# The rows of twelve k transfers and of a table divided anew among sixteen DMA engines, in a fused linear attention and spectral mixing kernel

## The chip, the cores and the metric

The kernel runs on one core of a Trainium2 chip. The core has a matrix engine (PE, with its weight loads PEld), a vector engine (DVE), a scalar engine (ACT), GpSimd (POOL) and SyncE (SP), and sixteen DMA engines that move data between HBM and on-chip memory. Time is device microseconds (us) of one execution, the median of several.

## The reference

For 8 batches, 8 heads, 576 positions and a head width of 64 (model width 512), in float32:

```python
def phi(x):
    return np.where(x > 0, x, np.exp(x) - 1.0) + 1.0
kv  = einsum('bhsd,bhse->bhde', phi(k), v);  z = phi(k).sum(over positions)
x   = einsum('bhsd,bhde->bhse', phi(q), kv) / (einsum('bhsd,bhd->bhs', phi(q), z) + 1e-6)
# heads side by side: x is (8, 576, 512)
X   = rfft(x, over positions);  Y = 0
Y[:, :64] = complex product of X[:, m] with (w_r[m] + i*w_i[m]) for the 64 lowest modes m
u   = x + irfft(Y)
out = u + maximum(u @ w_ch, 0)
```

w_r and w_i are 64 matrices of 512 x 512 each, so the weights are 134 MB of float32; q, k and v are 9.4 MB each. The output is 9.4 MB.

## The kernel before

**Stage one: attention and the forward transform.** For each batch `load(b)` (L172) brings q, k and v as one 128-row tile each: row r holds 2 x 1152 float32 numbers, converted to float16 on the way, so each row lands as two pieces of 2304 bytes. All of them but q of batch 0 go out on POOL's queue. `exps` (ACT) and `features` (DVE) form phi, `turn_q` and `sum_kv` (PE) transpose q and sum k times v, `form_x` divides by the denominator, and `transform` and `place_x` make the 64 modes. `load(b + 2)` is called at the top of batch b, and each of the tags q16, k16 and v16 has two buffers, so the loads of batch b + 2 wait until batch b has used its tile.

**The table.** The cosine and sine table is not loaded whole: FROWS = 576 // 4 - 63 = 81 of its rows come from HBM on SP's queue (L182), and `fold_table` (L330) makes rows 64 to 127 and a fifth block from rows 0 to 80 with matmuls whose k range is `slice(0, FROWS)`. Each row of the transfer is 4 x 128 float16, 1024 bytes.

**Weights.** `w_load` (L99) brings two modes of w_r and two of w_i in turn as 128 rows of 32 KB float32, which land as 16 KB bfloat16, on POOL's queue too. The first goes out in two halves of 64 rows between the loads of batches 3 and 5 (`next(pending)`, L467), four more follow the loads of batch 7, then the 512 x 512 matrix w_ch (`wch16`, L657), then one at a time, each when the PE has finished with the buffer that it takes (L106, two buffers of tag "w" and three of "wp"). `w_load_last` (L115) cuts the last modes into pieces, the last of them 64 KB.

**Stage two: one matrix pair after the other.** `mode_block(p)` multiplies the modes of all batches with weight tile p (L525, sixteen matmuls of 128 x 512), and between these blocks the PE and the other engines do rows of the inverse transform, the channel product and so on out of a list of work (`work_slot`).

**The end.** `last_pair` (L626) takes the last pieces as they land (L644). After them come a short chain of transposes, matmuls and copies (L1185 to L1210) and the last sums of each output tile (L1043), with stores on SP's queue.

**What the steps of the change touch.** `SHARES` (L170) says how a k tile's 128 rows are cut into transfers: batch 3 into 15, 63 and 50 rows, batch 5 into 5, 77, 35 and 11, every other tile into one transfer of 128. The loop at L186 issues one transfer per part. L68 and L182 set the table's rows.

Of the kernel before, what the change touches and what calls it, by code (L numbers as in the profile page):

```python
# [20 lines left out]
def _dft_consts(S: int, NM: int):  # L21

    m = np.arange(NM)
    s_cols = np.concatenate([4 * np.arange(128) + jj for jj in range(4)] + [512 + np.arange(NP)])
    s_rows = np.concatenate([s_cols, s_cols[512:]]).reshape(5, 128).T
    ang = 2.0 * np.pi * s_rows[:, :, None] * m / S
    by_four = np.concatenate([m[g::4] for g in range(4)])
    fwd = np.concatenate([np.cos(ang)[:, :, by_four], -np.sin(ang)[:, :, by_four]], axis=2)

    return fwd.astype(np.float16)  # L30
# [3 lines left out]
def kernel(  # L34
# [10 lines left out]
    nc = tc.nc  # L45
# [6 lines left out]
    NJJ = 4  # L52
# [12 lines left out]

    fwd_np = _dft_consts(S, NM)
    FROWS = S // 4 - 63
    fwd_dr = nc.inline_tensor(np.ascontiguousarray(fwd_np[:FROWS, :4]), name="dft_fwd")  # L68

    const = ctx.enter_context(tc.tile_pool(name="const", bufs=1, side="right"))  # L70
    xpool = ctx.enter_context(tc.tile_pool(name="xpool", bufs=1, side="right"))
# [3 lines left out]
    fwd_sb = const.tile([128, 5, 2 * NM], F16, name="fwd_sb")  # L75
# [17 lines left out]
    pin = tc.keep_in_program_order  # L93
# [73 lines left out]

    qT_all = [q_tile(f"qT{b}") for b in range(B)]
    raw, phi, x16s, xfs = {}, {}, {}, {}
    SHARES = {("k", 3): (15, 63, 50), ("k", 5): (5, 77, 35, 11)}  # L170

    def load(b):  # L172
        for nm, src in (("q", q), ("k", k), ("v", v)):
            rows_in = src[b].rearrange("h s d -> (h s) d").rearrange(
                "(hp r j) d -> r hp (j d)", r=128, j=2 * NJ
            )
            if (nm, b) == ("q", 0):
                for c in range(2):
                    t = sA.tile([128, 2, NJ * Dh], F32, tag="x16", bufs=2, name=f"q32_{c}")
                    pin(nc.sync.dma_start(out=t, in_=rows_in[:, :, c * NJ * Dh : (c + 1) * NJ * Dh]))  # L180
                    raw[nm, b, c] = t
                pin(nc.sync.dma_start(out=fwd_sb[0:FROWS, 0:NJJ, :], in_=fwd_dr.ap()))  # L182
                continue
            t = sA.tile([128, 2, 2 * NJ * Dh], F16, tag=f"{nm}16", bufs=2, name=f"{nm}16_{b}")
            r0 = 0
            for n in SHARES.get((nm, b), (128,)):  # L186
                pin(nc.gpsimd.dma_start(out=t[r0 : r0 + n], in_=rows_in[r0 : r0 + n]))
                r0 += n
            raw[nm, b] = t
# [259 lines left out]
    def set_diagonal(k: int, of=slice(0, B), copies=(nc.vector.tensor_copy,)):  # L449
        for g in range(4):  # L450
            rows = slice(32 * g, 32 * g + 32)
            src = xt[rows, of, :, k : XK : NQ - 1].rearrange("p b c t -> p c t b")
            pin(copies[g % len(copies)](out=xz[k % 2][rows, :, :, g, of], in_=src))  # L453

    load(0)
    load(1)
    ones_where(id16, -1, 1, 0)
    make_turns()
# [4 lines left out]
    for b in range(B):  # L463
        if b + 2 < B:
            load(b + 2)
            if b % 2 == 1:
                next(pending)  # L467
            if b == 2:
                pin(nc.gpsimd.memset(xz[0], 0.0))
        turn_q(b, 0)  # L470
        turn_q(b, 1)
        if b == 0:
            fold_table()
        sum_kv(b)
        if b + 1 < B:
            for _ in features(b + 1):
                pass
        if b + 2 < B:
            exps(b + 2)
        for jj in range(NJJ + 1):  # L480
            form_x(b, jj)
            if b == 0 and jj == 0:
                make_place()
            if b > 1 and jj == 1:
                place_x(b - 2)
            if b > 0 and jj in (2, 3):
                transform(b - 1, jj - 2)
        if b > 0:
            transform(b - 1, 2)
            transform(b - 1, 3)  # L490
# [245 lines left out]
    def x_of(t: int):  # L736
        if t < B * NJJ:
            return x_main[t // NJJ][:, t % NJJ, :]
        i = t - B * NJJ
        return x_tail[i // 2][:, i % 2, :]  # L740
# [234 lines left out]
    for b in range(B):  # L975
        pairs += [(b * NJJ, b * NJJ + 1), (b * NJJ + 2, b * NJJ + 3)]
        if b % 4 == 3:
            k = b // 4
# [251 lines left out]
    for i, t in enumerate(pairs[0]):  # L1230
# [4 lines left out]
                out=x_of(t), in0=accs[0][:, i], scalar=0.0, in1=x_of(t), op0=ALU.max, op1=ALU.add  # L1235
# [60 lines left out]
```

## Time and profile before

| what | us |
|---|---|
| median of 3 runs (lowest, highest) | 417.94 (417.76, 418.09) |
| the profiled execution, in all | 417.94 |
| its span, first to last instruction | 416.2 |
| PE busy / DVE busy / ACT busy / POOL busy | 304.5 / 243.7 / 148.5 / 51.9 |
| last mark of the first weight tile in halves (batch 3 of the loads) | 43.7 |
| last mark of v of batch 7, the last q, k, v transfer | 82.3 |
| first and last mark of the last weight piece | 383.1, 386.1 |
| span after the last mark | 30.1 |

A mark is a step of a transfer's semaphore. The trace holds sixteen of them for each transfer, one for each DMA engine that finished its share. They do not carry an engine's number. It also holds each DMA packet with its start, duration, bytes and queue, again without an engine's number.

| transfer | its sixteen marks in order, us |
|---|---|
| v, batch 2 | 28.08 28.11 28.16 28.19 28.21 28.22 28.26, 28.57 28.61 28.65 28.67 28.72 28.73 28.75 28.76, 29.68 |
| v, batch 3 | 35.88 35.91 35.98 35.98 36.02 36.07, 36.47, 37.01 37.11 37.12 37.15 37.19, 38.04, 38.15, 38.78 38.91 |
| last weight piece | 383.12 383.61 384.18 384.41 384.50 384.51 384.57 384.89 384.94 385.31 385.67 385.74 385.81 385.82 385.93 386.11 |

Queue 0 in the profile is POOL's transfers, queue 1 SP's, and the two "instruction" queues bring the program itself: queue 8 in packets of 16 KB, queue 14 in packets of 8 KB. A DMA share of the span is the time of all sixteen engines together.

### The profile page before, as it was taken

How to read it: one execution, taken by the hardware profiler on the slowest of the kernel's cores; microseconds unless marked ns; L12 is line 12 of the kernel's file. 1: busy time of each engine (PE TensorE's matmuls, PEld its weight loads, DVE VectorE, ACT ScalarE, POOL GpSimd, SP SyncE). 2: the span in 40 equal slices, each digit the busy share in tenths (PEclk: the TensorE clock that was granted, in tenths of full speed). 3: DMA queues.
4: the chain of work that ended last, by engine and by line, in shares of the span. 5: the costliest groups of instructions: out<-in, count | busy, mean ns of one | idle time of the engine just before them, and what ended most of it. 6: DMA issues, size and time to landing. Idle time of an engine off the chain costs nothing.

```text
span 416.2 us, 6713 instructions
## 1 busy us (share of the span) xinstructions
PE 304.5 (73%) x2767; PEld 171.4 (41%) x2767; DVE 243.7 (59%) x542; ACT 148.5 (36%) x220; POOL 51.9 (12%) x91
## 2 busy tenths in 40 slices
PE   0269799999583466576665466988978887887993
PEld 0167677777341233233332233443433333452431
DVE  3779978995732654557474442555455644722795
ACT  4667787864300001000000112244443442322583
POOL 6233423100110000000000000000100000230200
PEclk9999955788688558666666679789999999999997
DMA  8999999999999999999999999999999999999698
GB/s 216 211 211 217 208 221 202 226 217 213 217 213 216 217 219 219 211 218 219 216 219 211 219 217 217 219 212 217 218 216 222 209 219 217 213 212 195 216 402 344
DMA packets 16652, 92.84 MB, mean 223 GB/s; under 512 B 2054, under 2 KB 2807, under 8 KB 12335
## 3 DMA queue, kind: packets, MB, share of 16 engines
q0 software_dynamic: 12816, 81.70, 94.3%
q1 hardware_dynamic: 3806, 10.73, 6.8%
q8 instruction: 21, 0.34, 0.3%
q14 instruction: 9, 0.07, 0.0%
HBM read 163.66 MB, written 9.44 MB: 416 GB/s over the span
## 4 chain that ended last, share of the span: by engine, by line
DMA 53%; PE 26%; DVE 12%; ACT 3%; issue 3%; POOL 2%; DVEq 0%; ACTq 0%; POOLq 0%
DMA w<-in_moe_w_r_dram 33%; DMA w<-in_moe_w_i_dram 16%; PE P L525 9%; PE kvp L264 5%; DVE x_main L1043 3%; DMA k<-in_k_dram 3%; DVE x L300 3%; PE qTp L244 3%; PE eps L906 2%; PE xf L434 2%; DVE xz L453 1%; PE num L158 1%; ACT qT L251 1%; ACT ke L210 1%; DVE rd L297 1%
## 5 line engine op out<-in xcount | busy, mean ns | idle before, releaser
L525 PE MATMUL P<-w,xz 128*64 128x512 bf16 x480 | 82.9, 507 | 51.6 <-DMA w<-in_moe_w_r_dram 24.6
L525 PEld LDWEIGHTS <-xz 128*64 128x64 bf16 x480 | 39.1, 138 | 84.8 <-issue 72.6
L536 ACT CAST ys<-P 128x512 f16<-128x512 f32 x8 | 4.7, 585 | 115.6 <-PE P L525 115.6
L906 PE MATMUL eps<-wch,xTw 128*128 128x512 f16 x144 | 37.5, 385 | 3.8 <-DVE xTw L898 3.8
L887 DVE TENSOR_TENSOR x_main<-ya,x_main 128x512 f32<-128x512 f32 x32 | 21.9, 688 | 28.5 <-PE ya L883 28.2
L889 ACT CAST x16w<-x_main 128x512 f16<-128x512 f32 x32 | 19.8, 618 | 44.2 <-DVE x_main L887 43.3
L453 DVE COPY xz<-xt 32x384 bf16<-32x384 bf16 (+2 forms) x62 | 31.4, 507 | 2.1 <-ACT xt L419 1.2
L264 PE MATMUL kvp<-vpad,ke 32*128 32x130 f16 x576 | 23.4, 265 | 8.3 <-ACT qT L251 8.3
L837 PE MATMUL nw<-kv_diag,qT 128*128 128x130 f16 (+1 forms) x160 | 21.7, 261 | 10.3 <-DVE x_main L850 4.4
L914 ACT CAST E<-eps 128x512 f16<-128x512 f32 (+1 forms) x40 | 21.1, 539 | 22.1 <-PE eps L906 22.1
L534 DVE CAST ys<-P 128x512 f16<-128x512 f32 x10 | 6.9, 691 | 33.3 <-PE P L525 33.3
L264 PEld LDWEIGHTS <-ke 32*128 32x128 f16 x576 | 21.8, 117 | 9.7 <-issue 9.4
L244 PE MATMUL qTp<-id,qe 128*128 128x128 f16 x144 | 16.8, 310 | 11.3 <-DVE qe L228 9.6
L106 POOL DMA_DIRECT2D w<-in_moe_w_i_dram x15 | 8.0, 532 | 136.0 <-PE P L525 82.5
L106 POOL DMA_DIRECT2D w<-in_moe_w_r_dram x16 | 8.7, 545 | 124.5 <-PE P L525 114.9
L300 DVE TENSOR_TENSOR x<-num,rd 128x512 f16<-128x512 f32 x32 | 22.1, 691 | 1.1
L837 PEld LDWEIGHTS <-qT 128*128 128x128 f16 (+1 forms) x160 | 13.3, 125 | 22.6 <-issue 13.2
L898 DVE COPY xTw<-xTp 128x512 f16<-128x512 f16 x36 | 14.9, 416 | 9.8 <-PE xTp L896 9.7
L158 PE MATMUL num<-kv_sb,qT 64*128 64x65 f16 (+1 forms) x320 | 16.1, 220 | 6.1 <-DVE x L300 3.9
L251 ACT COPY qT<-qTp 128x1152 f16<-128x1152 f16 x16 | 19.5, 1282 | 2.6 <-PE qTp L244 2.0
L244 PEld LDWEIGHTS <-qe 128*128 128x128 f16 x144 | 14.6, 146 | 12.4 <-DVE qe L228 10.0
L848 DVE RECIPROCAL rdw<-nw 128x4 f32<-128x4 f32 (+1 forms) x40 | 7.0, 176 | 20.8 <-PE nw L837 20.4
(162 smaller groups left out, 501.0 us busy)
## 6 DMA issues: line engine op xcount, KB each, us to landing
w<-in_moe_w_i_dram POOLq DMA_DIRECT2D x15, 2048.0 KB, 17.0
w<-in_moe_w_r_dram POOLq DMA_DIRECT2D x14, 2048.0 KB, 15.5
out_dram<-x_main SPq DMA_DIRECT2D x14, 512.0 KB, 3.2
v<-in_v_dram POOLq DMA_DIRECT2D x8, 576.0 KB, 14.0
q<-in_q_dram POOLq DMA_DIRECT2D x7, 576.0 KB, 12.7
k<-in_k_dram POOLq DMA_DIRECT2D x6, 576.0 KB, 12.6
w<-in_moe_w_r_dram POOLq DMA_DIRECT2D x2, 1024.0 KB, 16.6
w<-in_moe_w_r_dram POOLq DMA_DIRECT2D x4, 512.0 KB, 11.9
```

Source lines behind the costliest of these rows:

```text
L158: mm = nc.tensor.matmul(num[hpo][orow, c0 : c0 + 65], qT[rows, hpp, h2, cols], kv_sb[rows, hpp, h2, :])
L244: nc.tensor.transpose(qT_ps[:, j], phi["q", b][:, c, j].rearrange("p o d -> p (o d)"), id16,)
L251: nc.scalar.copy(out=qT[:, :, c * NJ : (c + 1) * NJ], in_=qT_ps.rearrange("p j x -> p x j"))
L264: nc.tensor.matmul(kv_ps[:, h2, 0:130], phi["k", b][r0 : r0 + 32, j // NJ, j % NJ].rearrange("p o d -> p (o d)"), vp[r0 : r0 + 32, :, j, 0 ...
L300: nc.vector.tensor_tensor(out=dst.rearrange("p (o c d) -> p o c d", o=2, c=4), in0=nv[:, :, :, 0:64], in1=rden.unsqueeze(3).broadcast_to([ ...
L453: pin(copies[g % len(copies)](out=xz[k % 2][rows, :, :, g, of], in_=src))
L525: nc.tensor.matmul(P[c : c + width, :], x, w[:, dc, :], start=first, stop=last, tile_position=(0, c), skip_group_check=True,)
L837: nc.tensor.matmul(num[c][orow, h2 * 130 : h2 * 130 + 130], qT[:, c, h2, rows_of(jj, BASE[b % 2])], kv_diag[:, b, c, h2].rearrange("p o n ...
L887: pin(nc.vector.tensor_tensor(out=x, in0=acc, in1=x, op=ALU.add))
L889: pin(nc.scalar.copy(out=x16w[t], in_=x))
L906: nc.tensor.matmul(e_ps, xT[:, c, :], wch16[:, c, :], start=(c == 0), stop=(c == NDC - 1))
L914: pin(nc.scalar.copy(out=dst, in_=e_ps[:, cols]))
```

## The change

The table's transfer takes 96 rows in place of 81 (81 rounded up to a multiple of 16). `fold_table` still reads rows 0 to 80. The k tile of batch 3 is cut into four parts (18, 6, 100, 4) in place of three, that of batch 4 into four (20, 88, 2, 18) in place of one, and that of batch 5 into four others (15, 22, 84, 7). Nothing else differs. POOL issues 90 listed operations in place of 86; SP, PE, DVE and ACT issue the same ones as before.

```diff
     FROWS = S // 4 - 63
-    fwd_dr = nc.inline_tensor(np.ascontiguousarray(fwd_np[:FROWS, :4]), name="dft_fwd")
+    LROWS = -(-FROWS // 16) * 16
+    fwd_dr = nc.inline_tensor(np.ascontiguousarray(fwd_np[:LROWS, :4]), name="dft_fwd")
...
-    SHARES = {("k", 3): (15, 63, 50), ("k", 5): (5, 77, 35, 11)}
+    SHARES = {("k", 3): (18, 6, 100, 4), ("k", 4): (20, 88, 2, 18), ("k", 5): (15, 22, 84, 7)}
...
-                pin(nc.sync.dma_start(out=fwd_sb[0:FROWS, 0:NJJ, :], in_=fwd_dr.ap()))
+                pin(nc.sync.dma_start(out=fwd_sb[0:LROWS, 0:NJJ, :], in_=fwd_dr.ap()))
```

## The prediction

> **What bounds the kernel now.** I read first the DMA rows of the page, then its queues, then who waits for whom, then the chain that ended last.
>
> ```profile
> span 416.2 us, 6713 instructions
> ...
> DMA  8999999999999999999999999999999999999698
> ...
> q0 software_dynamic: 12816, 81.70, 94.3%
> q1 hardware_dynamic: 3806, 10.73, 6.8%
> q8 instruction: 21, 0.34, 0.3%
> q14 instruction: 9, 0.07, 0.0%
> ```
>
> The sixteen DMA engines are full from the first slice to the 37th. Instruction packets are 0.3% of all DMA time, but each falls on one engine.
>
> ```profile
> POOL w L106 <- PE P L525: 197.4, 21, 26.8
> ...
> PE P L525 <- DMA w<-in_moe_w_i_dram: 25.5, 10, 6.6
> PE P L525 <- DMA w<-in_moe_w_r_dram: 24.6, 11, 4.9
> ```
>
> ```profile
> 349.37 17.05 DMA w<-in_moe_w_i_dram
> 366.46 1.93 PE P L525 x16
> 368.40 0.29 issue
> 368.69 2.73 POOL w L122 x5
> 371.41 0.19 issue
> 371.60 13.84 DMA w<-in_moe_w_i_dram
> 385.49 0.36 PE yt L644 x8
> ```
>
> ```profile
> 386.15 0.26 PE L644 MATMUL yt<-xs,w 128*128 128x16 bf16 x4
> ...
> 386.45 0.22 DVE L652 CAST Y<-yt 128x64 f16<-128x64 f32 x1 [3.01 <-PE yt L644]
> ```
>
> In the second stage the PE waits for weights (25.5 + 24.6 us), not the weights for room: POOL's long waits at L106 end well before the queue runs dry. The transfer issued at 349.37 follows one whose earliest engine ends at 353.77 (its first mark), 4.4 us later. The last four matmuls of the last weights start at 386.15, 0.04 us after the last mark, 386.11. From there 30.1 us follow that the change doesn't touch. So the time is the last mark of the last piece plus 30.1 us, and the last mark belongs to the DMA engine with most to do. The sixteen last marks have a mean of 384.97: perfect division would be worth 1.14 us, 0.27% of the time, and no more.
>
> **How rows fall on engines.** I number the engines from the one that takes the first row of the first k part of batch 3. From v of batch 2 to v of batch 3 each engine moves 16 rows of q and v besides its share of k. Row packets between completion packets in that stretch come in counts of 2, 14, 10 (1, 7 and 5 rows), or with one of them zero. 15 rows as 15 x 1, 63 as 9 x 7 and 50 as 10 x 5, each part beginning at the engine after the last of the one before (mod 16), give 13 rows to engines 0 and 1, 12 to 15, 8 to 2-7 and 6 to 8-14. A row costs 2.787 us / 8 = 0.348 us (a step of one whole tile between marks). The marks of v of batch 3 agree: six at 35.88-36.07 and one at 36.47 (6 rows), five at 37.0-37.2 (8), 38.15 (12), 38.78 and 38.91 (13); 38.04 is one of 8 rows that took the 16 KB instruction packet at 26.00, whose step was 3.705 us instead of 2.79. In batch 5 the same reading gives 8, 7, 6, 12, 12 and 8 rows to engines 0-1, 2-3, 4-6, 7, 8 and 9-15. So a part goes to as many engines as the largest number up to 16 that divides its rows. The Trainium skill says the same in "DMA: Bandwidth & Descriptors", section "Why a DMA increments its semaphore by 16 and not by 1"; the trace agrees in all seven parts (1, 7, 5, then 1, 7, 5, 1 rows for an engine).
>
> The table's 81 rows go as 9 x 9: in v of batch 2 seven marks lie at 28.08-28.26 (mean 28.17), eight at 28.57-28.76 (mean 28.68). That is 0.51 us for 9 rows, 0.057 each, and the nine are engines 0-8, since the one late mark among those with 6 rows (36.47) must be engine 8.
>
> **Who is last, and why.** From 92 us on the packets can be strung together, since each starts within 20 ns of the end of the one before on its engine; this gives sixteen strings, with their instruction packets. A 16 KB packet costs 1.0 us (a string with two ends 2.07 us further than one with none), an 8 KB packet 0.48 us (four cost 1.91). Eight strings take the 16 KB packets in a fixed turn. By their marks at 82-92 us six are engines 9-14 and two are of 4-6. The 8 KB ones fall on three strings: two that by their marks are engines 2 and 3 (one of them has four, from 96.0 to 358.0 us) and one of engines 0 and 1 (at 67.6 and 301.3). The last mark, 386.11, is one of 4-6 with three 16 KB packets (26.0, 96.1, 301.9).
>
> **The change part by part.** Over batches 3, 4 and 5 (before, batch 4 is 8 rows each), by the rule above:
>
> ```
> engine   k rows before -> after   table rows      change us        last mark before   estimate after
> 0, 1     13+8+8=29   12+10+9=31   9 -> 6   +0.70-0.17=+0.53   385.31, 385.74     385.84, 386.27
> 2, 3      8+8+7=23   12+ 3+9=24   9 -> 6   +0.35-0.17=+0.18   383.61, 385.82     383.79, 386.00
> 4         8+8+6=22   12+ 4+9=25   9 -> 6   +1.04-0.17=+0.87   one of three:
> 5, 6      8+8+6=22   12+ 4+4=20   9 -> 6   -0.70-0.17=-0.87   383.12 384.94 386.11
> 7         8+8+12=28  12+10+8=30   9 -> 6   +0.70-0.17=+0.53   384.89             385.42
> 8         6+8+12=26  12+10+8=30   9 -> 6   +1.39-0.17=+1.22   384.18             385.40
> 9-12      6+8+8=22    2+10+8=20   0 -> 6   -0.70+0.34=-0.36   at most 385.93     at most 385.57
> 13, 14    6+8+8=22    1+10+9=20   0 -> 6   -0.70+0.34=-0.36   (these six)
> 15       12+8+8=28   10+10+9=29   0 -> 6   +0.35+0.34=+0.69   384.51             385.20
> ```
>
> The string that is last now drops to 385.24 if it is engine 5 or 6. What is late next is the engine of 0 and 1 that carries two 8 KB packets: 386.27, or +0.16 against 386.11.
>
> Four more parts (8 to 12): the two extra parts of batch 3 show their price between the marks of v of batches 2 and 3. Engines 9-14 took 7.83 us for 22 rows, 7.66 at 0.348, so 0.17 too much; engines 0 and 1 took 10.1 for 29 rows, 10.09, so nothing. Four more cost 0 to 0.34 us; I take 0.1, near the row of the engines that will be last. On POOL each part is one issue more, 0.56 to 0.85 us. v and the half weight tile behind them are issued 1.7 us (three extra issues) later in batch 4. This costs nothing, since between issue and landing of k lie 7.9 us at least; without that cover it would be 1.7 us. Between issue and dry engines the margin is smallest at q of batch 7 (issued 66.33, earliest engine done 70.74): 4.4 us. The k tile of batch 4 is complete when its last engine is: 22 rows since batch 3 and 6 table rows in place of 21 and 9, 0.18 us later, again under the queue's cover.
>
> ```profile
> L187 POOL DMA_DIRECT2D k<-in_k_dram x13: 557/713/853, 1.3 to 68.5; - x13
> ...
> DMA to landing us min/median/max: 7.9/11.3/15.2
> ```
>
> SP's table transfer is one issue before and after, in front of nothing until the stores at 388 us.
>
> Sum: +0.16 + 0.1 = +0.26 us, span 416.5. The profiled execution took 417.94 in all, the median of the runs, so 418.2.
>
> One rule speaks against this change. The Trainium skill's page "DMA: Bandwidth & Descriptors", section "Latency and other measured facts", has DMA engines 7 and 15 usually slower than others; the change gives 7 thirty rows and 15 twenty-nine. Here the trace doesn't agree: from 92 us on, strings without instruction packets took 293.45 to 293.67 us, those two 293.45 and 293.63. By the rule they would set the end; by the row they stay 0.8 us or more ahead of it.
>
> **The rivals.**
>
> *Slower: the last engine now is engine 4.* Three engines had equal rows so far (4, 5, 6), and the trace before can't part them by rows. If the string with three 16 KB packets is 4, it moves from 386.11 to 386.98, with the parts +0.97, so 418.9. It decides only in that case. Against it: the strings' turn goes, after two of 4-6, through the six of 9-14, and this string is the second of the two; if the turn follows the numbers, 4 can't be second. For it: that turn by numbers is only guessed.
>
> *Slower: an instruction packet more on 0, 1, 7 or 8.* These now have 30 or 31 rows, 385.4 to 386.3. If a 16 KB packet falls on engine 0 or 1, the end is 386.27 + 1.0 + 0.1, +1.3, so 419.2. Against it: in 21 such packets none did.
>
> *No gain or loss at all.* If 8 KB packets don't fall on 0 and 1 in most runs, the two end at 385.84 and the last is the other 8 KB engine, 386.00: -0.1 + 0.1 = 0, so 417.9.
>
> *Faster.* Only if the 16 strings level out: 384.97 and 0.3 us for the 15 extra table rows and the parts, -0.8, so 417.1. Against it: engines 0 and 1 without any packet are at 385.84 by rows alone.
>
> *Slower: rows dealt by another rule.* If each part went over all sixteen engines, a sixteenth of its rows rounded up for each until they are used up, engine 0 would have 9 + 8 + 10 rows before and 11 + 11 + 10 after, five more, +1.7 us, 419.7, if it is last. The marks of batch 3 speak against it: by it no engine gets 13 rows. The Trainium skill names this dealing in the section on the increment by 16, as an exception for some transfers of GpSimd's queue; the trace does not agree for the parts of before, and of those of the change it shows none yet.
>
> **How the numbers follow.** A measurement of this kernel can tell about 0.2% (0.84 us) from no change. The chances: forecast 0.47; no gain or loss 0.2; engine 4 last 0.1; packet on a heavy engine 0.08; other dealing 0.03; levelled out 0.12. The forecast and "no gain or loss" lie within 0.2%. Levelled out has its centre on the bound, -0.8, so half of its chance counts as faster, 0.06, and half as same: 0.73. Slower are three rivals, 0.21, the first of them just beyond 418.78. The range goes from levelled out, 417.1, to the packet on a heavy engine, 419.2; it takes in the parts' 0 to 0.34 and leaves out the other dealing. The forecast's own range is 417.9 to 418.5.
>
> **What would show it.** Marks of v of batch 5 in the new profile should show two engines with 31 rows of k, three with 29 or 30 and eleven with 20 to 25, and no group of seven early marks from the table. The last piece's marks should end within 386.0 to 386.6, with the last string one without 16 KB packets; the first mark of the last piece should rise from 383.1. A last mark near 387, with three 16 KB packets on its string, shows engine 4. The span after the last mark should stay 30.1: if it doesn't, or if the DMA row shows a gap between 40 and 110 us, the cover on POOL's queue was not there and the prediction is wrong.

## The result, and the profile after

| | before | after |
|---|---|---|
| median of 22 runs each, us (lowest to highest) | 417.89 (417.70 to 418.22) | 418.56 (418.37 to 418.81) |
| ratio (95% interval) | | 1.0015 (1.0009 to 1.0021) |
| median span of these kernels' runs, us | 416.2 | 416.5 |
| time of a run less its span, mean, us (lowest to highest) | 1.73 (1.69 to 1.79, 30 runs) | 2.05 (1.99 to 2.11, 22 runs) |
| last mark of the last weight piece, profiled execution | 386.11 | 386.25 |
| mean of that piece's sixteen marks | 384.94 | 385.05 |

The change makes the kernel slower by 0.67 us (0.16%), and the fourth row says where to look: some 0.3 us of it lie inside the span (the time from the first to the last instruction), and 0.32 outside, before the first instruction or after the last.

The page of the kernel after (its lines stand one further down than before, so L107 is the former L106, L526 the former L525): first the span, the DMA engines' busy share in 40 slices, and the DMA queues with packets, MB and share.

```profile
span 416.4 us, 6720 instructions
...
DMA  8999999999999999999999999999999999999698
...
q0 software_dynamic: 12944, 81.70, 94.3%
q1 hardware_dynamic: 3828, 10.75, 6.8%
q8 instruction: 21, 0.34, 0.3%
q14 instruction: 8, 0.07, 0.0%
```

The row of nines is the same as before, digit for digit: the engines are full to the 37th slice. POOL's queue moves the same 81.70 MB, in 128 packets more. The table's 15 rows add 0.015 MB on SP's queue. The waits of the kernel after (us in total, times, longest):

```profile
POOL w L107 <- PE P L526: 208.4, 22, 29.0
...
PE P L526 <- DMA w<-in_moe_w_i_dram: 27.2, 12, 8.7
...
PE P L526 <- DMA w<-in_moe_w_r_dram: 23.2, 12, 5.1
```

The PE waits 50.4 us for weights, 50.1 before. PE, DVE and ACT are busy for as long as before, within 0.5 us; POOL is busy for 55.0 us in place of 51.9, with 95 listed operations in place of 91. Waits for semaphores are not among the listed operations: of these ACT has three more than before, which matters further down. The chain that ended last (start, us, what):

```profile
349.51 17.05 DMA w<-in_moe_w_i_dram
366.56 0.04 issue
366.60 1.93 PE P L526 x16
368.54 0.29 issue
368.82 2.15 POOL w L123 x4
370.98 13.95 DMA w<-in_moe_w_i_dram
384.92 0.05 issue
384.97 0.36 PE yt L645 x8
```

It is the chain of before, 0.14 us later at its head (349.51 for 349.37). Its end, in the timeline:

```profile
386.30 0.26 PE L645 MATMUL yt<-xs,w 128*128 128x16 bf16 x4
...
386.59 0.23 DVE L653 CAST Y<-yt 128x64 f16<-128x64 f32 x1 [3.03 <-PE yt L645]
```

The last four matmuls start at 386.30, 0.05 us after the last mark, where they started at 386.15 before. From the last mark to the end of the span it is 30.10 us (416.35 less 386.25), as before.

The sixteen marks of four transfers of the kernel after show how the rows fell on the DMA engines:

```
v, batch 2      after  28.4 28.4 28.5 28.5 28.5 28.5 28.5 28.5 28.6 28.6 28.6 28.6 28.7 28.7 28.8 | 29.6
v, batch 3      after  34.9 35.2 35.5 35.5 35.7 36.0 | 37.7 | 38.2 38.2 38.3 38.3 38.3 38.4 38.4 39.1 39.4
v, batch 5      after  57.3 57.4 57.5 57.6 | 58.4 58.5 58.6 58.6 58.6 59.1 59.1 | 60.4 60.6 60.7 60.9 61.0
last piece      after  383.74 383.76 384.28 384.38 384.46 384.60 385.13 385.28 385.32 385.39 385.42
                       385.51 385.58 385.76 385.94 386.25
```

The table's group of seven early marks is gone: fifteen marks of v of batch 2 lie within 0.43 us, without a gap, as they should when all engines have 6 table rows. In v of batch 3 there are six engines with 1 or 2 rows of k, one with 10 and nine with 12, as forecast, and in v of batch 5 five late engines (29 to 31 rows) and eleven others. From 92 us on the packets can be strung together, each joined to the one that starts as it ends, so that a string is the work of one DMA engine. The string that ends last has no 16 KB instruction packet and one of 8 KB (at 299.3 us). It is also the last of the sixteen at the start of the strings (92.47 us, the last mark of the first whole weight tile), as an engine with 31 rows must be: one of engines 0 and 1, as forecast.

### The profile page after: what moved, and what is told of

Same layout as the page of the kernel before. It is cut to its first block, busy times and chain, and to the rows that moved or that the text cites. A ratio compares the mean times of both kernels' runs of the same rounds, so it can differ in the third digit from the quotient of the medians.

```text
span 416.4 us, 6720 instructions
## 1 busy us (share of the span) xinstructions
PE 304.9 (73%) x2767; PEld 172.8 (42%) x2767; DVE 243.7 (59%) x542; ACT 149.0 (36%) x220; POOL 55.0 (13%) x95
## 3 DMA queue, kind: packets, MB, share of 16 engines
q0 software_dynamic: 12944, 81.70, 94.3%
## 4 chain that ended last, share of the span: by engine, by line
DMA 63%; PE 18%; DVE 10%; issue 3%; ACT 2%; POOL 2%; DVEq 0%; POOLq 0%
DMA w<-in_moe_w_r_dram 36%; DMA w<-in_moe_w_i_dram 19%; PE P L526 8%; DMA k<-in_k_dram 5%; DVE x_main L1044 3%; DMA q<-in_q_dram 3%; PE kvp L265 3%; DVE x L301 3%; PE qTp L245 2%; PE xf L435 1%; DVE xz L454 1%; PE num L159 1%; PE eps L907 1%; ACT qT L252 1%; PE acc L961 1%
## 5 line engine op out<-in xcount | busy, mean ns | idle before, releaser
L526 PE MATMUL P<-w,xz 128*64 128x512 bf16 x480 | 83.9, 512 | 52.0 <-DMA w<-in_moe_w_i_dram 25.3
L526 PEld LDWEIGHTS <-xz 128*64 128x64 bf16 x480 | 40.8, 140 | 85.2 <-issue 73.7
L107 POOL DMA_DIRECT2D w<-in_moe_w_i_dram x15 | 8.0, 533 | 136.3 <-PE P L526 93.7
L107 POOL DMA_DIRECT2D w<-in_moe_w_r_dram x16 | 8.7, 545 | 124.0 <-PE P L526 114.8
```

The costliest lines, as they stand in the source:

```text
L526: nc.tensor.matmul(P[c : c + width, :], x, w[:, dc, :], start=first, stop=last, tile_position=(0, c), skip_group_check=True,)
```

## The experiments

Every kernel below is the kernel before with one edit, unless it says otherwise. "Outside" is the time of a run less its span; the span of a run is known to 0.1 us. The comparisons are with the kernel before on the same chip. A diff that shows only the new `SHARES` leaves out the line of before that it replaces.

**The two halves of the change, each alone.** With the table in 96 rows and the parts as before:

```diff
-    fwd_dr = nc.inline_tensor(np.ascontiguousarray(fwd_np[:FROWS, :4]), name="dft_fwd")
+    LROWS = -(-FROWS // 16) * 16
+    fwd_dr = nc.inline_tensor(np.ascontiguousarray(fwd_np[:LROWS, :4]), name="dft_fwd")
...
-                pin(nc.sync.dma_start(out=fwd_sb[0:FROWS, 0:NJJ, :], in_=fwd_dr.ap()))
+                pin(nc.sync.dma_start(out=fwd_sb[0:LROWS, 0:NJJ, :], in_=fwd_dr.ap()))
```

> Theory (the engine with the most work sets the end): the table costs 6 rows x 0.057 us on every engine instead of 9 on engines 0-8 and none on 9-15, so the last string of before (385.9 after -0.17) is passed by one of 9-14 (385.93 + 0.34 = 386.27): last mark +0.16 us, median 418.05 against 417.89. Rival (the number of k parts makes the loss): the parts are those of before, so 417.9.

417.98 us against 417.97, ratio 1.0000 (0.9992 to 1.0009), span 416.2, last mark 386.05, outside 1.73. The table alone changes nothing that can be measured, and the theory's +0.16 us did not come: the rival had the number. In this trace four strings, each with two 16 KB packets from 92 us on, end at marks of 385.96 to 386.05, and none reaches 386.27. The one that was last before (packets now at 98.6 and 302.0 us) is still last, at 386.05 in place of 386.11, where the theory had it fall by 0.17. Why it did not fall is not shown.

With the new parts and the table as before:

```diff
-    SHARES = {("k", 3): (15, 63, 50), ("k", 5): (5, 77, 35, 11)}
+    SHARES = {("k", 3): (18, 6, 100, 4), ("k", 4): (20, 88, 2, 18), ("k", 5): (15, 22, 84, 7)}
```

> Theory: engines 0 and 1 get two rows more and keep 9 table rows: 385.74 + 0.70 = 386.44, and 0.1 for four parts more: +0.43, median 418.3; last string one without 16 KB packets. Rival (parts): the whole loss is here, 418.56.

418.76 us, ratio 1.0016 (1.0007 to 1.0025). The span, 416.7 in the median, is 0.45 over that of before, the forecast +0.43. The last mark of the profiled execution is 386.46, of a string without 16 KB packets and with one of 8 KB (300.8 us), as expected. So the 96-row table is worth 0.2 us once engines 0 and 1 are last (416.5 with it), where 0.17 was worked out from 3 rows of 0.057 us; both spans are known to 0.1 us only. The total is 0.46 above the expected 418.3, and 0.32 of that is outside the span: 2.05 here too. The unforecast part comes with the parts, not with the table.

**What a part costs.** First no parts at all:

```diff
-    SHARES = {("k", 3): (15, 63, 50), ("k", 5): (5, 77, 35, 11)}
+    SHARES = {}
```

> No k tile is cut, every engine has 24 rows. Theory: the strings with three 16 KB packets gain two rows, 386.11 + 0.70 = 386.81, five parts less are worth 0.05: +0.65, median 418.5; last string one with three 16 KB packets. Rival (parts, 0.67 us / 4 = 0.17 each): five parts less, -0.8, median 417.05.

418.37 us, ratio 1.0012 (1.0003 to 1.0021), span 416.7 in the median, outside 1.72: near the theory's 418.5, and far from the rival's 417.05. The last four strings here carry two 16 KB packets each (at 147.2 and 373.0, 99.9 and 322.7, 93.9 and 302.1, 114.5 and 349.4 us) and the strings without packets from 92 us on end 2.1 us or more before the last: instruction packets set the end, and the parts of before bought about 0.5 us against that.

Then twelve parts with rows that divide evenly, so that no engine's rows change:

```diff
+    SHARES = {("k", 3): (48, 32, 32, 16), ("k", 4): (48, 32, 32, 16), ("k", 5): (48, 32, 32, 16)}
```

> Batches 3, 4 and 5 cut into four parts each, all multiples of 16 rows, so every engine has 24 rows as undivided, but twelve parts. Theory: a part costs an engine its completion packet, 0.02 us: nine parts more than undivided, +0.2, median 418.7. Rival (parts): nine times 0.17 more than undivided, +1.5.

419.06 us, ratio 1.0027 (1.0017 to 1.0037); span 417.0, outside 2.05. Against no parts, nine parts more cost 0.3 us of span (the theory 0.2, the rival 1.5), 0.03 each; four are 0.13, where the forecast took 0.1. Another 0.33 came outside the span, as in the kernel after. Here one more thing shows: a weight tile issued at 294.01 us, 1.7 us before the earliest engine was done, came 0.8 us late on that engine, so part of the 0.3 may not be the parts' own price.

**The rule by which rows are dealt, and the cover.**

```diff
+    SHARES = {("k", 3): (17, 15, 96)}
```

> Only batch 3's k tile is cut, into 17, 15 and 96 rows: engine 0 takes 23 of them, every other one 7. Theory (a part goes to the largest divisor up to 16, and the engine with most rows sets the end): engine 0 has 39 rows over the three batches, a string without 16 KB packets that ended at 383.6 undivided comes to 383.6 + 15 x 0.348 + 0.33 = 389.1, 2.8 us after undivided's 386.34; median 418.37 + 2.8 = 421.2. Rival (rounded-up sixteenths for 17 and 15): engine 0 gets 2 + 1 + 6 = 9, no change, 418.4.

421.51 us in the median of four runs, ratio 1.0079 (1.0064 to 1.0095). The rule holds: fifteen marks of v of batch 3 lie between 36.2 and 38.2 and one at 42.2, 5.2 us (15 rows of 0.348) after the 37.0 that an engine of its kind has without parts. So 17 rows went to a single engine. The total, too, is only 0.3 us from the theory's 421.2, but that is in part luck: the theory had one late engine, and here the last marks are all late, 388.1 to 390.1, the mean 389.2 in place of 384.9 without parts. The other fifteen engines lost time too, in these stretches (us from the start, DMA share and GB/s are the last two columns), first of this kernel:

```profile
core 0: us, PE busy (x) PEld busy (x) DVE busy (x) ACT busy (x) POOL busy (x), PEclk, DMA share, GB/s
120.00:150.00 30.00, 14.54 (x103) 6.77 (x99) 12.03 (x43) 0.58 (x1) 0.53 (x1) 0.78 1.05 219
150.00:170.00 20.00, 12.10 (x75) 6.57 (x73) 9.73 (x25) 1.99 (x5) 1.06 (x2) 0.67 0.96 189
170.00:200.00 30.00, 19.89 (x124) 10.20 (x120) 17.63 (x55) 1.28 (x3) 2.06 (x4) 0.69 1.00 210
```

and of the kernel before:

```profile
120.00:150.00 30.00, 15.99 (x109) 8.23 (x110) 14.13 (x49) 0.58 (x1) 0.64 (x2) 0.70 1.05 219
150.00:170.00 20.00, 11.44 (x70) 5.92 (x70) 10.56 (x32) 2.62 (x7) 1.06 (x2) 0.76 1.02 218
170.00:200.00 30.00, 19.74 (x120) 10.29 (x120) 17.82 (x55) 0.58 (x1) 1.58 (x3) 0.67 1.01 215
```

Between 150 and 170 us the queue ran dry: 189 GB/s for 218. A weight tile (four modes of w_r or four of w_i) is issued when the PE is done with the one whose buffer it takes, and the PE waits for the slowest engine; the margin is from that issue to the first mark of the tile in flight:

```
issue     first mark of the tile before   margin   step to its own first mark
150.49    151.12                          0.63     11.34
160.22    162.46                          2.24     10.30
170.88    172.76                          1.88     10.75
180.52    183.51                          2.99      9.69
```

A full step is 9.69 us, so the first three came 1.65, 0.61 and 1.06 us late: a tile must be issued 2.3 to 2.9 us ahead (margin plus delay). In the kernel before, the tightest issue is that at 195.49, 3.1 us ahead of the first mark at 198.6; in the kernel after, some are 2.9 ahead (147.43, 157.10), and the steps that follow are still 9.7.

**A division of my own,** with six parts, and the table in 96 rows, meant to put the light engines under the 16 KB packets:

```diff
+    SHARES = {("k", 3): (24, 66, 38), ("k", 4): (104, 24)}
```

> Table of 96 rows; k of batch 3 as 24, 66, 38, of batch 4 as 104, 24, batch 5 whole: 26 rows for engines 0-1, 31 for 7-8, 18 for 6, 20 for 9-11, 24 for the rest. Theory with the part's price as measured (0.07 us an engine, six parts instead of eight): if the strings with three 16 KB packets are 6, 9, 10 and 11, the last mark is 385.8, median 417.6, faster than both. If they are others of 9-14, the ones with 24 rows come to 386.5 and it is 418.3.

418.69 us, ratio 1.0019 (1.001 to 1.0028), span 417.0, outside 1.73: slower than before, by the span alone. Fifteen of the last marks lie between 383.6 and 386.1, and one at 386.9. The guess that the engines with three 16 KB packets are 6, 9, 10 and 11 does not hold, and the second case, 418.3, is 0.4 us short as well; which engine is the last was not settled. (The 0.07 us for a part in the expectation is the difference of two medians, 0.69 us over nine parts, of which 0.33 lies outside the span.)

**What lies outside the span.** The 0.33 us appeared with twelve parts, not with eight. Six kernels ask what it goes with. Ten parts:

```diff
+    SHARES = {("k", 3): (48, 32, 32, 16), ("k", 4): (64, 64), ("k", 5): (48, 32, 32, 16)}
```

> Even rows in ten parts. What lies outside the span was 1.72 us with 3 parts, 1.73 with 8 and 2.06 with 12. If it is a step with the number of transfers or instructions on POOL, this shows on which side ten lie: 1.7 or 2.06. If it grew with each part it would be 1.9.

One run, 419.04 us, span 417.2, outside 1.84: between the two. Then no parts, but twelve memsets on POOL's stream:

```diff
-    SHARES = {("k", 3): (15, 63, 50), ("k", 5): (5, 77, 35, 11)}
+    SHARES = {}
...
+    scrap = const.tile([128, 1], F32, name="scrap")
+    for _ in range(12):
+        pin(nc.gpsimd.memset(scrap, 0.0))
```

> Undivided with twelve small memsets on POOL, no transfer more. If the step outside the span comes with POOL's instructions of any kind, 2.06 us outside; if with transfers, 1.72.

One run, 418.42 us, span 416.7, outside 1.72. More instructions on POOL alone don't bring it. Sixteen parts:

```diff
+    SHARES = {("k", b): (48, 32, 32, 16) for b in (3, 4, 5, 6)}
```

> The k tiles of batches 3 to 6 cut into four parts each (48, 32, 32, 16): 16 parts, all with even rows. Read is what lies outside the span: 1.72 us with 3 and 5 parts, 1.73 with 8, 1.84 in the one run with ten, 2.06 with twelve. If every transfer on POOL's queue above 8 costs the same, 0.083 us each, it is 1.73 + 8 x 0.083 = 2.39 with sixteen. If it is a step that twelve have reached, it stays 2.06. The span: twelve such parts measured 417.0 in the median; four more at 0.04 to 0.06 each give 417.2.

419.15 us, ratio 1.0028 (1.0016 to 1.0039); outside 2.03 in the mean of 8 runs, 1.97 to 2.06. It does not grow with each part: twelve have already reached the full step. The span is 417.1, 0.1 over that of twelve. Twelve parts of v in place of k:

```diff
+    SHARES = {("v", b): (48, 32, 32, 16) for b in (3, 4, 5)}
```

> Not k but the v tiles of batches 3 to 5 in four parts each (48, 32, 32, 16); k undivided. POOL issues as many transfers as with twelve parts of k. If what lies outside the span goes with the number of POOL's transfers, it is 2.06 us as with twelve parts of k; if it is something of the k loads alone, 1.72. Span 417.0 as with k (the last v transfer of a batch lands later by the same few hundredths).

418.72 us, ratio 1.0018 (1.0006 to 1.0029); span 417.0, outside 1.72 in the mean of 8 runs, 1.68 to 1.77. This fells the theory of POOL's transfers: there are as many as with twelve parts of k, and the step is gone. Nine table transfers on SP's queue:

```diff
-                pin(nc.sync.dma_start(out=fwd_sb[0:FROWS, 0:NJJ, :], in_=fwd_dr.ap()))
+                for r in range(0, FROWS, 9):
+                    pin(nc.sync.dma_start(out=fwd_sb[r : r + 9, 0:NJJ, :], in_=fwd_dr.ap()[r : r + 9]))
```

> The parts of k as before (8 parts), but the table's 81 rows go out as nine transfers of 9 rows on SP's queue. Eight more transfers in all, none of them on POOL's queue. If what lies outside the span goes with POOL's transfers alone, it stays 1.73 us; if it goes with all transfers of the program, it rises to 2.06 at least. Span: the nine start one engine after the other, so every engine gets 5 or 6 table rows in place of 9 or none: engines 0 and 1 0.17 to 0.23 us lighter, the last string not among them; 416.2 as before, within 0.2.

418.22 us, ratio 1.0007 (0.9996 to 1.0019); span 416.2, outside 1.95 in the mean of 8 runs, but spread from 1.72 to 2.21, far more than in any other kernel. So it is not only parts of k. One thing of the expectation did not come: the marks of v of batch 2 still part into two groups (six at 28.16 to 28.39, eight at 28.62 to 28.79, two later), as with one transfer of 81 rows; in the kernel after, with 6 rows on every engine, there is no such gap. So the nine transfers on SP's queue did not spread their rows evenly. Of the explanations for the time outside, what was left is the length of the program, since every kernel up to 6715 instructions had 1.72 to 1.74, and those from 6716 on had more. So the kernel with twelve memsets is given 24, for 6727 instructions:

```diff
-    for _ in range(12):
+    for _ in range(24):
```

> k undivided, and 24 memsets of one number per partition on POOL's stream in place of 12: 6727 instructions in all. What lies outside the span was 1.72 to 1.74 us in all kernels of 6703 to 6715 instructions, 1.84 in the one run with 6716, and 1.95 to 2.05 in the mean with 6720 to 6733. If it goes with the length of the program as such, it is 2.05 here. If it goes with transfers and the instructions that wait for them (310 and 311 listed on ACT in the kernels with 1.84 and 2.05, 306 here), it stays 1.72. Span as with k undivided: 416.7.

418.41 us, ratio 1.0009 (0.9998 to 1.0021); span 416.65 in the median, outside 1.72 in the mean of 8 runs, 1.69 to 1.78. The length of the program is not it. The first line of this kernel's page, against that of the kernel after above (6720 instructions, outside 2.05):

```profile
span 416.7 us, 6727 instructions
```

What still goes with it in most kernels is the number of parts of k, and with it the number of instructions with which ACT waits at the line of the exponential. In the kernel before, in that after, and in the one with twelve parts of v, in this order (count, then shortest, median and longest in ns):

```profile
L210 ACTq EVENT_SEMAPHORE  x14: 17/38/38, 24.7 to 79.7; - x14
```

```profile
L211 ACTq EVENT_SEMAPHORE  x17: 17/38/1399, 24.7 to 80.0; - x17
```

```profile
L210 ACTq EVENT_SEMAPHORE  x12: 17/17/38, 24.8 to 79.0; - x12
```

| kernel | parts of k, batches 3 to 5 (sixteen: 3 to 6) | POOL transfers | instructions | ACT waits at that line | outside, mean (runs) |
|---|---|---|---|---|---|
| no parts | 3 | 72 | 6703 | 12 | 1.72 (11) |
| 24 memsets, no parts | 3 | 72 | 6727 | 12 | 1.72 (8) |
| twelve parts of v | 3 | 81 | 6714 | 12 | 1.72 (8) |
| before | 8 | 77 | 6713 | 14 | 1.73 (30) |
| ten parts | 10 | 79 | 6716 | 16 | 1.84 (1) |
| after | 12 | 81 | 6720 | 17 | 2.05 (22) |
| twelve even parts | 12 | 81 | 6720 | 17 | 2.05 (8) |
| sixteen even parts | 16 | 84 | 6724 | 18 | 2.03 (8) |
| nine table transfers | 8 | 77 | 6733 | 14 | 1.95 (8) |

The first eight rows go with the parts of k and with ACT's waits alike; the last goes with neither, unless the waits that the nine table transfers add elsewhere act likewise. Whether waits alone, without transfers, bring the step was not tried. Nor is it known whether the step lies before the first instruction or after the last. The traces record semaphore steps past the last instruction, but the last of them comes 1.90 us after it in the kernel before and with twelve even parts, and 1.93 in the kernel after and with no parts, so the 0.33 us do not show there.

## Why the prediction was right, and where it was not

The forecast was 418.2 us, with 417.9 to 418.5 as its own range and 417.1 to 419.2 over all cases. The 418.56 measured lies in the whole range, but 0.06 us above the forecast's own. The mechanism in the span came out as told; the rest of the sum, taken as unchanged, did not.

**What bounds the kernel: right.** The engines stayed full, the last matmuls start 0.05 us after the last mark, and 30.1 us follow, in both kernels. The mean of the sixteen last marks before is 384.94, not 384.97, so perfect division would be worth 1.17 us in place of 1.14.

**The rule for rows: right,** also for the parts that the trace before did not hold, and for 17 rows on one engine. The Trainium skill's rule in "DMA: Bandwidth & Descriptors", section "Why a DMA increments its semaphore by 16 and not by 1", by which the number of engines used divides the rows, agrees with the 5.2 us measured for 15 rows.

**Who is last: right.** One of engines 0 and 1, at 386.25 (forecast 386.27); the other's string ends at a mark of 385.76 (385.84), and the former last string with its 16 KB packets at 95.4 and 302.4 us at 385.28 (385.24, if it is engine 5 or 6). The forecast's figures leave out the parts' 0.1 us; with it the last mark was to be 386.37. One execution of each kernel was profiled, and the spans of single runs differ by 0.5 us, so an agreement to 0.02 us is in part luck; that these engines are last is not. The price of an instruction packet was read against the longest string without one (293.67 us). The other five strings without packets took 293.45 us, and against these a 16 KB packet costs 1.1 us, and one 8 KB packet alone (301.3 us) 0.32, its own duration. The sum does not hang on it.

**The parts' price: right within its bounds.** 0.1 was taken from between 0 and 0.34; even parts cost 0.13 for four. The forecast span was 0.26 over that of before; the profiled one is 0.13 over it, the medians 0.3. Because of the late weight tile, 0.13 is an upper value rather than a measured price.

**The table: right where it counted.** It is worth 0.2 on engines 0 and 1 (0.17), as the two kernels with and without it show. The table alone, though, did not move the last string as its rows would have it.

**The cover on POOL's queue: held, but its tightest place was named wrongly.** The text put the smallest margin at q of batch 7, 4.4 us. The weights from 147 to 245 us are issued with only 3.1 to 3.4 to spare before, 2.9 to 3.3 after, and 2.3 to 2.9 are needed. An engine that is some us late takes from that, since the PE waits for it. Nothing was lost in the kernel after, but little was left.

**What lies around the span: mis-sized.** The forecast said that "the profiled execution took 417.94 in all", added the change of the span alone, and so took the 1.73 us outside as constant, without a reason given. It measured 2.05 in the kernel after. That +0.32 is most of the distance between the forecast 418.2 and the 418.56 measured, and about half of the whole effect. Here it comes with the new parts of k and not with the 96-row table. It goes neither with the length of the program nor with the number of POOL's instructions or transfers, and nine table transfers raised it too; its cause stays open.

**The rivals.** Engine 4 last: no, the last string has no 16 KB packet. A packet on a heavy engine: from 92 us on no 16 KB packet fell on the two heaviest. No gain or loss: the condition, that no 8 KB packet falls on 0 and 1, was not met (one at 299.3). Levelled out: the last mark stands 1.2 us over the mean, as before. Dealing by rounded-up sixteenths: no, by the marks of batch 3 and by the 17 rows. Engines 7 and 15 were not last: the last string is of 0 or 1, and in the kernel after the strings without instruction packets took 293.45 to 293.57 us. The Trainium skill's rule that those two are usually slower ("DMA: Bandwidth & Descriptors", section "Latency and other measured facts") does not show here.

## What to carry to other kernels

Where sixteen DMA engines are full from start to end, the last mark belongs to one engine, and which one can be forecast from rows, packets and a dealing rule. It came out here for the change and for its parts alone; with the table alone and with the six parts it was off by 0.2 and 0.4 us or more. A rearrangement can gain at most the distance between the last mark and the mean (here 1.2 us), and it pays for each part it adds. A division that looks lighter on the engine that was last is to be reckoned on the one that becomes last: here it went from 386.11 to 386.25. And a forecast of the span is not yet one of the time: at a few tenths of a us compare what lies outside it, too.

## What the runs showed of the hardware that was not expected

- Outside the span lie 1.72 to 1.74 us in kernels with 3 to 8 parts of k, and 2.03 to 2.05 in those with 12 and 16; with 8 parts and nine table transfers it is 1.95, between 1.72 and 2.21. Its cause stays open.
- A weight transfer issued less than 2.3 to 2.9 us before the earliest engine is done leaves that engine idle. With one engine 5.2 us behind the others the margin fell to 0.6 us, and all sixteen lost time: the mean of the last marks rose by 4.3 us.
- A transfer of 17 rows went to one DMA engine, which was 5.2 us late for its 15 rows more than an undivided tile gives it. Nine table transfers of 9 rows on SP's queue left the marks in two groups, as one transfer of 81 rows does.
